# Order of the last sums and layout of the stores in a one-token decode block

## The chip, the cores and the metric

The kernel runs on one core of a Trainium2 chip. The core has a matrix engine (PE; its weight loads, PEld, are listed apart from its matmuls), VectorE (DVE), ScalarE (ACT), GpSimd (POOL) and SyncE (SP), which here issues all transfers between HBM and the on-chip memory SBUF. Matmuls write to PSUM, from which DVE or ACT copy. The metric is the device time of one execution in microseconds.

## The reference

A decode step for 8 sequences of one token each, model width 1024, all in float32. Two residual blocks follow each other:

```python
h  = x + A(layernorm(x), k_cache, v_cache, wq, wo)
h2 = h + B(layernorm(h), w_gate, w_up, w_down)

# A: 32 query heads of 128, 4 key/value heads, the last W = 1024 positions of a cache of 4096
q = (x @ wq) in heads;  p = softmax(q k^T * 128 ** -0.5);  A = (p v) @ wo
# B: width 3584
B = (gelu_tanh(x @ w_gate) * (x @ w_up)) @ w_down
```

The 8 tokens are few against the weights and the cache, some 111 MB that are read once.

## The kernel before, in words

**Tiling.** The 8 tokens are the stationary side of nearly every matmul, the weights the moving side. A matmul takes 32 stationary columns, and four of them, in the four groups of 32 columns of the PE array, run beside each other and write rows 0-31, 32-63, 64-95 and 96-127 of a PSUM bank. As there are 8 tokens, each stands four times in the 32 columns (`CP = 4` copies). The order of these columns is (copy, token): column 8 r + b is copy r of token b, so each group's rows in PSUM hold the 8 tokens four times over, copy after copy.

**Loads.** Two buffers of 64 KB in each partition take the weights in turn (`load`, line 119): two halves of wq, of K, of V and of wo, four blocks of w_gate and w_up, then w_down. A load is issued by SyncE when the matmuls that read the buffer before are done (`free`).

**The attention half** (lines 202-330): layernorm, query projection, scores, softmax, values, output projection. The output projection works in pairs: groups 0 and 1 take an even row chunk of 128 rows (left and right 512 output columns), groups 2 and 3 the odd one, so that the bank holds two partial sums. `add2`, a stationary matrix of zeros and ones, adds the two halves in a matmul (line 326). The residual sum goes to `h_sb` (line 329), whose rows 0-7 are the tokens and whose other rows are zero.

**The feed-forward half.** `layernorm_t` (line 173) normalizes `h_sb`, transposes it, and copies it out four times over (line 198), which gives the stationary tiles `ht`. Lines 335-362 make gate and up products, GELU and the transposed product `at`: 28 chunks of 128 rows, each with its 32 columns. w_down has 28 row chunks as well. They arrive in pieces of 8, 8, 4, 4, 2 and 1 chunks (`PARTS`), and the last chunk in three blocks, 128, 64 and 64 columns of each quarter of the output (`ENDS`). All are issued by line 391.

**The last sums** (lines 394-435), which the change touches. With `TAIL = 4`, `first` is 24 and `last` 27:

1. Chunks 0 to 23 go in pairs into bank `ya` (line 397), 512 columns at a time.
2. DVE copies `ya` to `d1` in SBUF (line 404).
3. `add` (line 410) sends one operand to the final sums: eight matmuls of 128 columns, four into `acc` and four into `tb`. Group j has the output quarter j (256 columns), of which `acc` holds the first 128 and `tb` the others. In this order `add` is called for the residual (`spread` selects row b of `h_sb` for each column of token b; this call opens the sums), for chunks 24 and 25, for `d1` with `add2`, and for chunk 26.
4. Chunk 27 follows in its three end blocks (line 429). ACT copies `acc` to `o_fin` when the first block is in, DVE copies `tb` when the third is in (line 433), and SyncE stores each half (lines 436-437): 128 rows of 128 numbers, contiguous in the output.

The order on each engine is the order of the source. An engine runs its instructions in that order, and `Flow` (line 31) puts a semaphore wait ahead of one only if what it needs isn't known to be done. Each `matmul` call of the source is two matmul instructions and two weight loads in the trace.

Of the kernel before, what the change touches and what calls it, by code (L numbers as in the profile page):

```python
# [2 lines left out]
F32 = mybir.dt.float32  # L3
# [4 lines left out]
P = 128  # L8
B = 8
# [5 lines left out]
NC = D // P  # L15
NQ = 4
CP = 32 // B
QW = D // NQ
N = 512
SET = NQ * N  # L20
HB = B // 2
SETS = (NQ, DF // N - NQ)
# [2 lines left out]
PARTS = (8, 8, 4, 4, 2, 1)  # L25
HEAD = 16
ENDS = (128, 64, 64)
TAIL = 4


class Flow:
# [42 lines left out]
    def run(self, engine, make, *waits, mark=True):  # L74
        ins = self.start(engine, make, waits)
        if not mark:
            return None
        self.done[engine] += 1
        ins.then_inc(self.own[engine], 1)
        return self.own[engine], self.done[engine]  # L80

    def move(self, name, out, src, *waits, engine="sync"):
        s = self.sem(name)
        self.start(engine, lambda e: e.dma_start(out, src), waits).then_inc(s, 16)  # L84
        return s, 16


def decode_block(nc, x, wq, kt, v, wo, gu, dn, ends, outs):
# [9 lines left out]
    run, move = fl.run, fl.move  # L98
# [4 lines left out]
    def sb(name, *shape):  # L103
        return nc.alloc_sbuf_tensor(name, list(shape), F32).ap()
# [14 lines left out]
    def load(src, name, letters, **sizes):  # L119
# [9 lines left out]
    ta, tb, ya = bank("ta", N), bank("tb", N), bank("ya", N)  # L129
    acc = bank("acc", N)  # L130

    x_sb = sb("x_sb", B, D)
    wq_t = [load(wq[0], "wq0", "c n", c=NC)]
    x_in = move("x", x_sb, x)
# [3 lines left out]
    ident = sb("ident", P, P)  # L138
    z = run("gpsimd", lambda e: e.memset(ident, 0.0))
    id_ok = run("gpsimd", lambda e: e.affine_select(  # L140
        out=ident, in_=ident, compare_op=ALU.not_equal, fill=1.0, base=0,
        pattern=[[-1, P]], channel_multiplier=1), z)
# [4 lines left out]
    h_sb = sb("h_sb", P, D)  # L147
    zero = [run("gpsimd", lambda e, t=t: e.memset(t, 0.0)) for t in (*qz, h_sb)]

    spread = sb("spread", P, CP, B)  # L150
    run("gpsimd", lambda e: e.tensor_copy(
        spread, ident[:, 0:B].unsqueeze(1).to_broadcast([P, CP, B])), id_ok)

    add2 = sb("add2", P, 2, 32)
    consts = run("gpsimd", lambda e: e.tensor_add(
        add2.rearrange("p c m -> p (c m)"), ident[:, 0:2 * 32], ident[:, 2 * 32:4 * 32]))
# [3 lines left out]
        out=own, in_=ident.rearrange("p (a b h) -> p b a h", b=HB, h=REP), axis=AX.XY,  # L160
# [9 lines left out]
                id_ok, ready, clear, mark=(i == n - 1))  # L170
        return t, tok

    def layernorm_t(src, ready, name, clear):

        bn = sb(name + "_bn", B, D // N, 6)
        tok = None
        for i in range(D // N):
            tok = run("vector", lambda e, i=i: e.bn_stats(bn[:, i], src[:, i * N:(i + 1) * N]), ready)
        mv, ve, sd, r0, r1, r2, rs = (
            sb(f"{name}_{n}", B, k) for n, k in  # L180
            (("mv", 2), ("ve", 1), ("sd", 1), ("r0", 1), ("r1", 1), ("r2", 1), ("rs", 1))
        )
        tok = run("vector", lambda e: e.bn_aggr(mv, bn), tok)
        tok = run("vector", lambda e: e.tensor_scalar(ve, mv[:, 1:2], EPS, None, op0=ALU.add), tok)  # L184
        tok = run("scalar", lambda e: e.activation(sd, ve, AF.Sqrt), tok)  # L185
        tok = run("vector", lambda e: e.reciprocal(r0, sd), tok)

        tok = run("vector", lambda e: e.scalar_tensor_tensor(
            r1, r0, r0, ve, op0=ALU.mult, op1=ALU.mult), tok)
        tok = run("vector", lambda e: e.tensor_scalar(  # L190
            r2, r1, -0.5, 1.5, op0=ALU.mult, op1=ALU.add), tok)
        tok = run("vector", lambda e: e.tensor_mul(rs, r0, r2), tok)
        xn = sb(name + "_xn", B, D)
        tok = run("vector", lambda e: e.tensor_scalar(  # L194
            xn, src, mv[:, 0:1], rs, op0=ALU.subtract, op1=ALU.mult), tok)
        pt, tok = transposes(ta, xn, NC, tok, clear, B)
        xt = sb(name + "_t", P, NC, CP, B)
        tok = run("vector", lambda e: e.tensor_copy(  # L198
            xt, pt.unsqueeze(2).to_broadcast([P, NC, CP, B])), tok)
        return [xt[:, c].rearrange("p r b -> p (r b)") for c in range(NC)], tok  # L200

    xt, x_ok = layernorm_t(x_sb, x_in, "ln1", None)
    ta_free = x_ok


    q_ok = []
    for hf in range(2):
        w, w_in, wb = wq_t[hf]
        q_ps = (acc, tb)[hf]
        for c in range(NC):  # L210
            for j in range(NQ):
                tok = run("tensor", lambda e, c=c, j=j: e.matmul(  # L212
                    q_ps[32 * j:32 * j + 32, :], xt[c], w[:, c, j * N:(j + 1) * N],
                    start=(c == 0), stop=(c == NC - 1)),
                    w_in, x_ok, mark=(c == NC - 1 and j == NQ - 1))
        free[wb] = tok
        q_sb = sb(f"q{hf}", P, N)
        tok = run("vector", lambda e: e.tensor_scalar(q_sb, q_ps, scale, None, op0=ALU.mult), tok)
        acc_free = tok
        qt, tok = transposes(ta, q_sb, N // P, tok, ta_free)  # L220

        for s in range(2):
            ta_free = run("vector", lambda e, s=s: e.tensor_copy(
                qz[hf][:, s].rearrange("p (b m) -> p b m", b=B)[:, :, 0:REP].rearrange(
                    "p b (k i) -> p b k i", k=2),
                qt.rearrange("p i (s k m) -> p s m k i", s=2, k=2)[:, s, 0:B]), tok, zero[hf])
# [4 lines left out]
    for hf in range(2):  # L231
        s_ps = big[hf]
        k_t, k_in, wb = load(kt[hf], f"kt{hf}", "s b k", s=2, b=B)
        for b in range(HB):
            for k0 in range(0, W, N):
                for r in range(NQ):
# [3 lines left out]
                    tok = run("tensor", lambda e: e.matmul(  # L240
                        s_ps[32 * r:32 * r + 32, k0:k0 + N], qz[hf][:, s, c0:c0 + 32],
                        k_t[:, s, half * HB + b, k0:k0 + N],
                        start=(b == 0), stop=(b == HB - 1)), k_in, q_ok[hf], mark=end)
# [29 lines left out]
    ya_free = None  # L273
    o_ps = (acc, tb)
    for hf in range(2):
        p_sb, p_ok, share, sh_ok = ps[hf]
        pt = sb(f"pt{hf}", P, KC, P)
        p0, tok0 = transposes(ta, p_sb[:, 0:W // 2], KC // 2, p_ok, ta_free)
        ta_free = run("vector", lambda e: e.tensor_copy(pt[:, 0:KC // 2, :], p0), tok0)
        p1, tok1 = transposes(ya, p_sb[:, W // 2:W], KC // 2, p_ok, ya_free)  # L280
        ya_free = run("scalar", lambda e: e.copy(pt[:, KC // 2:KC, :], p1), tok1)
        v_t, v_in, wb = load(v[hf], f"v{hf}", "s c b d", s=2, c=KC, b=B)
        o3 = o_ps[hf].rearrange("p (b d) -> p b d", b=HB)
        for c in range(KC):
            for r in range(NQ):
                s, half = divmod(r, 2)
                tok = run("tensor", lambda e: e.matmul(  # L287
                    o3[32 * r:32 * r + 32], pt[:, c, 32 * r:32 * r + 32],
                    v_t[:, s, c, half * HB:(half + 1) * HB, :],
                    start=(c == 0), stop=(c == KC - 1)),  # L290
                    v_in, ta_free, ya_free, mark=(c == KC - 1 and r == NQ - 1))
        free[wb] = tok
        o_sb = sb(f"o{hf}", P, DH)
        tok = run("vector", lambda e: e.tensor_scalar(
            o_sb, o3[:, 0], share[:, 0:1], None, op0=ALU.mult), tok, sh_ok)
        for b in range(1, HB):
            tok = run("vector", lambda e: e.scalar_tensor_tensor(
                o_sb, o3[:, b], share[:, b:b + 1], o_sb, op0=ALU.mult, op1=ALU.add), tok)
        if hf == 0:
            o_first = (o_sb, tok)  # L300
        else:
            ta_free = heads_out(0, *o_first, ta_free)
# [22 lines left out]
    for ch in range(2):  # L325
# [2 lines left out]
            ya_free, consts, ps[0][1], mark=(ch == 1))  # L328
    h_ok = run("vector", lambda e: e.tensor_add(
        h_sb[0:B], x_sb, big[0][0:B]), tok, zero[2])  # L330
    ht, ht_ok = layernorm_t(h_sb[0:B], h_ok, "ln2", ta_free)
    ta_free = ht_ok


# [42 lines left out]
    def rows_of(q):  # L377
        return chunks(q)[1][:, 0]
# [10 lines left out]
    for i, (n, src) in enumerate(zip(ENDS, ends)):  # L389
        t = rows_of(last)[:, NQ * c0:NQ * (c0 + n)]  # L390
        blocks.append((c0, n, t, move(f"we{i}", t, src)))
        c0 += n

    for q in range(0, first, 2):
        for r in range(NQ):
            e2, ch = divmod(r, 2)
            tok = run("tensor", lambda e: e.matmul(  # L397
                ya[32 * r:32 * r + 32, :], at[:, q + e2, :],
                rows_of(q + e2)[:, ch * N:(ch + 1) * N],
                start=(q == 0), stop=(q == first - 2)),  # L400
                arrived[q + e2], at_ok[(q + e2) * P >= SETS[0] * N], ya_free,
                mark=(q == first - 2 and r == NQ - 1))
    d1 = sb("d1", P, N)
    d1_ok = run("vector", lambda e: e.tensor_copy(d1, ya), tok)


    cut = ENDS[0]
    halves = [(acc[:, 0:cut], 0, cut), (tb[:, 0:QW - cut], cut, QW)]
# [1 line left out]
    def add(lhs, rhs, *waits, start=False):  # L410

        for d_ps, a, b in halves:
            for j in range(NQ):
                run("tensor", lambda e: e.matmul(  # L414
                    d_ps[32 * j:32 * j + 32, :], lhs(j), rhs(j)[:, a:b], start=start, stop=False),
                    *waits, mark=False)

    add(lambda j: spread.rearrange("p r b -> p (r b)"), lambda j: h_sb[:, j * QW:(j + 1) * QW],
        h_ok, consts, start=True)
    for q in range(first, last):  # L420
        add(lambda j: at[:, q, :], lambda j: rows_of(q)[:, j * QW:(j + 1) * QW], arrived[q], at_ok[1])
        if q == first + 1:
            add(lambda j: add2[:, j // 2, :], lambda j: d1[:, (j % 2) * QW:(j % 2) * QW + QW], d1_ok)
    o_fin = sb("o_fin", P, QW)
    done = []
    for i, (c0, n, t, here) in enumerate(blocks):
# [5 lines left out]
        if c0 + n == b:  # L432
            make = (lambda e: e.copy(o_fin[:, a:b], d_ps)) if i == 0 else (
                lambda e: e.tensor_copy(o_fin[:, a:b], d_ps))
            done.append(run(("scalar", "vector")[i > 0], make, tok))
    sent = [move("out0", outs[0], o_fin[:, 0:cut], done[0]),
            move("out1", outs[1], o_fin[:, cut:QW], done[1])]
    for s, val in sent:
        nc.sync.wait_ge(s, val)

# [76 lines left out]
```

## Time and profile before

| | |
|---|---|
| time, median of three runs | 267.58 us (265.7, 267.58, 268.12) |
| profiled execution: time | 267.58 us |
| profiled execution: span, first to last instruction | 266.3 us |
| PE matmuls, weight loads | 990 and 990, busy 51% and 15% of the span |
| mean granted TensorE clock | 0.788 |
| bytes moved | 111.45 MB, mean 419 GB/s |
| instruction queue q8 | 8 packets, 0.13 MB |
| each of the two stores | 64 KB |

In the fences below, a row of the chain has its start, its length and what it was (a DMA tile, or an engine with tile and line). A row of the timeline has start, length, engine, line, operation, tiles, shapes and the number of instructions, and in brackets the engine's idle time before it and what ended it. A row of the windows has start:end, length, then for PE, PEld, DVE, ACT and POOL the busy time with instructions in brackets, the granted clock, the DMA share of 16 engines and GB/s. A row of the issues ends in KB and in the time from issue to landing. A row of a DMA queue has packets, MB, and the share of 16 engines' time in the stretch asked for.

### The profile page before, as it was taken

How to read it: one execution, taken by the hardware profiler on the slowest of the kernel's cores; microseconds unless marked ns; L12 is line 12 of the kernel's file. 1: busy time of each engine (PE TensorE's matmuls, PEld its weight loads, DVE VectorE, ACT ScalarE, POOL GpSimd, SP SyncE). 2: the span in 40 equal slices, each digit the busy share in tenths (PEclk: the TensorE clock that was granted, in tenths of full speed). 3: DMA queues.
4: the chain of work that ended last, by engine and by line, in shares of the span. 5: the costliest groups of instructions: out<-in, count | busy, mean ns of one | idle time of the engine just before them, and what ended most of it. 6: DMA issues, size and time to landing. Idle time of an engine off the chain costs nothing.

```text
span 266.3 us, 2117 instructions
## 1 busy us (share of the span) xinstructions
PE 136.2 (51%) x990; PEld 40.1 (15%) x990; DVE 23.5 (9%) x55; ACT 10.5 (4%) x15; POOL 3.2 (1%) x11
## 2 busy tenths in 40 slices
PE   0000986805905806807708409619319294783874
PEld 0000321201201302202102102112002021120223
DVE  0004010100010110300300100250000200010000
ACT  1002000000010110110000000020000000000000
POOL 4000000000000000000000000000000000000000
PEclk9999995965865965975957956956858859599599
DMA  8997999799979997999799989998999989999992
GB/s 315 473 473 320 473 473 455 335 463 473 463 335 463 465 463 345 465 453 473 345 453 463 465 354 443 463 473 354 436 404 465 473 362 436 448 418 421 433 391 70
DMA packets 3338, 111.45 MB, mean 419 GB/s; under 512 B 377, under 2 KB 889, under 8 KB 1153
## 3 DMA queue, kind: packets, MB, share of 16 engines
q1 hardware_dynamic: 3328, 111.31, 97.4%
q8 instruction: 8, 0.13, 0.2%
q14 instruction: 2, 0.01, 0.0%
HBM read 111.18 MB, written 0.13 MB: 418 GB/s over the span
## 4 chain that ended last, share of the span: by engine, by line
DMA 76%; PE 22%; SPq 1%; issue 0%; DVE 0%
DMA w<-gu 19%; DMA w<-wq 15%; DMA w<-kt 11%; DMA w<-v 11%; DMA w<-wo 11%; DMA w<-dn 8%; PE big L345 7%; PE tb L212 4%; PE tb L287 4%; PE ya L315 3%; PE big L240 3%; SPq L84 1%; PE acc L414 0%; PE tb L414 0%; PE tb L429 0%
## 5 line engine op out<-in xcount | busy, mean ns | idle before, releaser
L345 PE MATMUL big<-w,ln_t 128*32 128x512 f32 x224 | 36.7, 737 | 20.9 <-DMA w<-gu 20.9
L240 PE MATMUL big<-w,qz 128*32 128x512 f32 x128 | 18.1, 728 | 19.3 <-DMA w<-kt 19.3
L315 PE MATMUL ya<-w,ot 128*32 128x512 f32 x128 | 17.3, 701 | 20.3 <-DMA w<-wo 20.3
L168 PE MATMUL ta<-ident,ln_xn 8*128 8x8 f32 x16 | 2.0, 251 | 31.6 <-DVE ln_xn L194 31.6
L397 PE MATMUL ya<-w,at 128*32 128x512 f32 x96 | 13.6, 717 | 7.0 <-DMA w<-dn 7.0
L345 PEld LDWEIGHTS big<-w,ln_t 128*32 128x32 f32 x224 | 9.1, 133 | 47.1 <-issue 25.8
L287 PE MATMUL tb<-w,pt 128*32 128x512 f32 x64 | 9.5, 761 | 9.4 <-DMA w<-v 9.4
L287 PE MATMUL acc<-w,pt 128*32 128x512 f32 x64 | 9.0, 727 | 9.8 <-DMA w<-v 9.8
L212 PE MATMUL tb<-w,ln_t 128*32 128x512 f32 x64 | 9.8, 779 | 2.7 <-DMA w<-wq 2.7
L212 PE MATMUL acc<-w,ln_t 128*32 128x512 f32 x64 | 10.0, 797 | 0.5 <-DVE ln_t L198 0.5
L315 PEld LDWEIGHTS ya<-w,ot 128*32 128x32 f32 x128 | 4.9, 127 | 31.3 <-issue 31.3
L240 PEld LDWEIGHTS big<-w,qz 128*32 128x32 f32 x128 | 4.7, 131 | 32.1 <-issue 22.3
L168 PEld LDWEIGHTS ta<-ident,ln_xn 8*128 8x128 f32 x16 | 1.8, 213 | 32.5 <-DVE ln_xn L194 32.5
L356 DVE TENSOR_TENSOR hm<-ge,big 128x512 f32<-128x512 f32 (+1 forms) x2 | 1.4, 686 | 56.8 <-PE big L345 56.8
L397 PEld LDWEIGHTS ya<-w,at 128*32 128x32 f32 x96 | 3.2, 129 | 16.6 <-DMA w<-dn 8.8
L249 DVE TENSOR_REDUCE nmax<-big 128x1 f32<-128x1024 f32 x2 | 2.4, 1224 | 34.1 <-PE big L240 34.1
L287 PEld LDWEIGHTS tb<-w,pt 128*32 128x32 f32 x64 | 2.6, 135 | 15.7 <-issue 15.7
L287 PEld LDWEIGHTS acc<-w,pt 128*32 128x32 f32 x64 | 2.5, 131 | 15.7 <-issue 15.7
L251 ACT ACTIVATE p<-big,nmax 128x1024 f32<-128x1024 f32 x2 | 2.2, 1114 | 64.9 <-DVE nmax L249 64.9
L212 PEld LDWEIGHTS tb<-w,ln_t 128*32 128x32 f32 x64 | 2.4, 139 | 9.4 <-issue 6.5
L185 ACT ACTIVATE ln_sd<-ln_ve 8x1 f32<-8x1 f32 x2 | 0.4, 202 | 83.8 <-DVE ln_ve L184 83.8
L212 PEld LDWEIGHTS acc<-w,ln_t 128*32 128x32 f32 x64 | 2.4, 140 | 7.4 <-issue 6.8
(73 smaller groups left out, 51.1 us busy)
## 6 DMA issues: line engine op xcount, KB each, us to landing
w<-gu SPq DMA_DIRECT2D x2, 6144.0 KB, 22.4
w<-dn SPq DMA_DIRECT2D x2, 4096.0 KB, 19.2
w<-dn SPq DMA_DIRECT2D x2, 2048.0 KB, 17.3
w<-dn SPq DMA_DIRECT2D x1, 1024.0 KB, 21.6
w<-dn SPq DMA_DIRECT2D x1, 512.0 KB, 22.4
w<-ends SPq DMA_DIRECT2D x1, 256.0 KB, 22.5
w<-ends SPq DMA_DIRECT2D x2, 128.0 KB, 22.3
out<-o_fin SPq DMA_DIRECT2D x2, 64.0 KB, 2.4
```

Of the source, the lines that this page charges most:

```text
L84: self.start(engine, lambda e: e.dma_start(out, src), waits).then_inc(s, 16)
L168: tok = run("tensor", lambda e, i=i: e.transpose(t[:, i, :], src[:, i * P:(i + 1) * P], ident[:rows, :rows]), id_ok, ready, clear, mark=(i ...
L185: tok = run("scalar", lambda e: e.activation(sd, ve, AF.Sqrt), tok)
L212: tok = run("tensor", lambda e, c=c, j=j: e.matmul(q_ps[32 * j:32 * j + 32, :], xt[c], w[:, c, j * N:(j + 1) * N], start=(c == 0), stop=(c ...
L240: tok = run("tensor", lambda e: e.matmul(s_ps[32 * r:32 * r + 32, k0:k0 + N], qz[hf][:, s, c0:c0 + 32], k_t[:, s, half * HB + b, k0:k0 + N ...
L249: tok = run("vector", lambda e: e.tensor_reduce(out=nmax, in_=s_ps, axis=AX.X, op=ALU.max, negate=True), tok)
L251: p_ok = run("scalar", lambda e: e.activation(p_sb, s_ps, AF.Exp, bias=nmax, accum_out=tot), tok)
L287: tok = run("tensor", lambda e: e.matmul(o3[32 * r:32 * r + 32], pt[:, c, 32 * r:32 * r + 32], v_t[:, s, c, half * HB:(half + 1) * HB, :], ...
L315: tok = run("tensor", lambda e: e.matmul(ya[32 * r:32 * r + 32, :], ot[:, 2 * hf * REP + h + e2].rearrange("p r b -> p (r b)"), w[:, h + e ...
L345: tok = run("tensor", lambda e: e.matmul(pair[32 * j:32 * j + 32, s, :], ht[c], w[:, c, j * N:(j + 1) * N], start=(c == 0), stop=(c == NC ...
L356: tok = run("vector", lambda e: e.tensor_mul(hm[:rows], ge[:rows], pair[:rows, 1, :]), tok, g_ok)
L397: tok = run("tensor", lambda e: e.matmul(ya[32 * r:32 * r + 32, :], at[:, q + e2, :], rows_of(q + e2)[:, ch * N:(ch + 1) * N], start=(q == ...
```

## The change

`TAIL` becomes 2, so `first` is 26: chunks 24 and 25 join the pairs, and only chunks 26 and 27 go one by one. The residual is no longer the first of the final sums. It opens the pairs' sum instead, with two matmuls of 512 columns in groups 0 and 1 of `ya`, ahead of the first pair; groups 2 and 3 are opened by the first odd chunk. So `d1` now holds the residual and chunks 0 to 25. The final sums are opened by chunk 26, then take `d1` by `add2`, then the three end blocks.

The 32 columns of the second layernorm's output are in the order (token, copy), column 4 b + r, by an argument of `layernorm_t`; `spread` likewise. The first layernorm keeps (copy, token). In the final sums, rows 4 b of each group of 32 are then copy 0 of token b, and each store takes every fourth of the 128 rows: 32 rows of 128 numbers, 16 KB, into an output of 32 rows of 256.

```diff
-TAIL = 4
+TAIL = 2
...
-    spread = sb("spread", P, CP, B)
+    spread = sb("spread", P, B, CP)
     run("gpsimd", lambda e: e.tensor_copy(
-        spread, ident[:, 0:B].unsqueeze(1).to_broadcast([P, CP, B])), id_ok)
+        spread, ident[:, 0:B].unsqueeze(2).to_broadcast([P, B, CP])), id_ok)
...
-    def layernorm_t(src, ready, name, clear):
+    def layernorm_t(src, ready, name, clear, order):
...
-        xt = sb(name + "_t", P, NC, CP, B)
+        xt = sb(name + "_t", P, NC, CP * B)
         tok = run("vector", lambda e: e.tensor_copy(
-            xt, pt.unsqueeze(2).to_broadcast([P, NC, CP, B])), tok)
-        return [xt[:, c].rearrange("p r b -> p (r b)") for c in range(NC)], tok
+            xt.rearrange(f"p c ({order}) -> p c r b", b=B),
+            pt.unsqueeze(2).to_broadcast([P, NC, CP, B])), tok)
+        return [xt[:, c] for c in range(NC)], tok
-    xt, x_ok = layernorm_t(x_sb, x_in, "ln1", None)
+    xt, x_ok = layernorm_t(x_sb, x_in, "ln1", None, "r b")
...
-    ht, ht_ok = layernorm_t(h_sb[0:B], h_ok, "ln2", ta_free)
+    ht, ht_ok = layernorm_t(h_sb[0:B], h_ok, "ln2", ta_free, "b r")
...
+    for ch in range(2):
+        run("tensor", lambda e: e.matmul(
+            ya[32 * ch:32 * ch + 32, :], spread.rearrange("p b r -> p (b r)"),
+            h_sb[:, ch * N:(ch + 1) * N], start=True, stop=False), h_ok, consts, ya_free, mark=False)
     for q in range(0, first, 2):
         for r in range(NQ):
             e2, ch = divmod(r, 2)
             tok = run("tensor", lambda e: e.matmul(
                 ya[32 * r:32 * r + 32, :], at[:, q + e2, :],
                 rows_of(q + e2)[:, ch * N:(ch + 1) * N],
-                start=(q == 0), stop=(q == first - 2)),
-                arrived[q + e2], at_ok[(q + e2) * P >= SETS[0] * N], ya_free,
+                start=(q == 0 and e2 == 1), stop=(q == first - 2)),
+                arrived[q + e2], at_ok[(q + e2) * P >= SETS[0] * N],
                 mark=(q == first - 2 and r == NQ - 1))
...
-    add(lambda j: spread.rearrange("p r b -> p (r b)"), lambda j: h_sb[:, j * QW:(j + 1) * QW],
-        h_ok, consts, start=True)
     for q in range(first, last):
-        add(lambda j: at[:, q, :], lambda j: rows_of(q)[:, j * QW:(j + 1) * QW], arrived[q], at_ok[1])
-        if q == first + 1:
-            add(lambda j: add2[:, j // 2, :], lambda j: d1[:, (j % 2) * QW:(j % 2) * QW + QW], d1_ok)
+        add(lambda j: at[:, q, :], lambda j: rows_of(q)[:, j * QW:(j + 1) * QW],
+            arrived[q], at_ok[1], h_ok, start=(q == first))
+    add(lambda j: add2[:, j // 2, :], lambda j: d1[:, (j % 2) * QW:(j % 2) * QW + QW], d1_ok)
...
-    sent = [move("out0", outs[0], o_fin[:, 0:cut], done[0]),
-            move("out1", outs[1], o_fin[:, cut:QW], done[1])]
+    sent = [move("out0", outs[0], o_fin[0:P:CP, 0:cut], done[0]),
+            move("out1", outs[1], o_fin[0:P:CP, cut:QW], done[1])]
...
-    out = nc.dram_tensor("out", (P * QW,), F32, kind="ExternalOutput").ap()
-    cut = P * ENDS[0]
-    outs = [o.rearrange("(p n) -> p n", p=P) for o in (out[0:cut], out[cut:P * QW])]
+    out = nc.dram_tensor("out", (NQ * B, QW), F32, kind="ExternalOutput").ap()
+    outs = [out[:, 0:ENDS[0]], out[:, ENDS[0]:QW]]
```

More of the change, by code (lines that the diff above doesn't have):

```diff
@@ L511 @@
     r = run_bass_kernel_spmd(nc, [arrays], core_ids=[0])
-    flat = r.results[0]["out"].reshape(-1)
-    got = np.concatenate(
-        [flat[:cut].reshape(P, -1), flat[cut:].reshape(P, -1)], axis=1
-    ).reshape(NQ, CP, B, QW)[:, 0]
+    got = r.results[0]["out"].reshape(NQ, B, QW)
     return own(got.transpose(1, 0, 2)).reshape(B, 1, D)
```

## The prediction

> **What bounds the kernel now.** I read the page first: its totals, the chain that ended last, and the DMA queues.
>
> ```profile
> span 266.3 us, 2117 instructions
> PE 136.2 (51%) x990; PEld 40.1 (15%) x990; DVE 23.5 (9%) x55; ACT 10.5 (4%) x15; POOL 3.2 (1%) x11
> ...
> q8 instruction: 8, 0.13, 0.2%
> ...
> DMA 76%; PE 22%; SPq 1%; issue 0%; DVE 0%
> ```
>
> The weight stream ends last almost everywhere; PE is busy half the span. Every change lies in the last 30 us, so next comes the chain cut to its end.
>
> ```profile
> 237.91 21.58 DMA w<-dn
> ...
> 259.54 0.42 PE acc L414 x8
> ...
> 261.50 0.34 PE acc L429 x8
> 261.84 0.60 PE tb L429 x16
> 262.46 0.29 DVE o_fin L434
> ```
>
> The chain waits for rows 24 and 25 of w_down until 259.50, then is PE work until 261.84 + 0.60 = 262.44, one copy, and the store (which this view leaves out). The instructions of that stretch, in order of time:
>
> ```profile
> 257.02 1.92 PE L397 MATMUL ya<-w,at 128*32 128x512 f32 x16 [1.77 <-DMA w<-dn]
> 257.48 0.13 PEld L397 LDWEIGHTS ya<-w,at 128*32 128x32 f32 x4 [0.30 <-issue]
> 257.91 0.13 PEld L397 LDWEIGHTS ya<-w,at 128*32 128x32 f32 x4 [0.30 <-issue]
> ...
> 258.76 0.40 PE L414 MATMUL acc<-h_sb,spread 128*32 128x128 f32 x8
> ...
> 259.02 0.69 DVE L404 COPY d<-ya 128x512 f32<-128x512 f32 x1 [19.99 <-PE ya L397]
> 259.54 0.16 PEld L414 LDWEIGHTS acc<-w,at 128*32 128x32 f32 x8 [0.43 <-DMA w<-dn]
> ...
> 260.00 0.40 PE L414 MATMUL acc<-w,at 128*32 128x128 f32 x8
> ...
> 260.44 0.40 PE L414 MATMUL acc<-d,add 128*32 128x128 f32 x8
> ...
> 260.80 0.21 PEld L414 LDWEIGHTS acc<-w,at 128*32 128x32 f32 x8
> 260.88 0.40 PE L414 MATMUL acc<-w,at 128*32 128x128 f32 x8
> ...
> 261.41 0.16 PEld L429 LDWEIGHTS acc<-w,at 128*32 128x32 f32 x8 [0.19 <-DMA w<-ends]
> ...
> 261.80 0.44 PEld L429 LDWEIGHTS tb<-w,at 128*32 128x32 f32 x16 [0.23 <-DMA w<-ends]
> 261.91 0.27 ACT L433 COPY o_fin<-acc 128x128 f32<-128x128 f32 x1 [38.34 <-PE acc L429]
> 262.08 0.16 PEld L429 LDWEIGHTS tb<-w,at 128*32 128x32 f32 x8
> ```
>
> What to see: PE isn't late here. It waits for the first end block until 261.41 and for the second until 261.80; the first eight loads of the pair end at about 261.96, so the third block's eight, at 262.08, waited about 0.1 us for it. Loads and PE finish within a few tenths of each other. The copy of the pairs' sum (259.02 to 259.71) is done long before its use at 260.44. Last, the two stores: their issues, a view of each issue with its time to landing, the traffic from 262.7 to 266.3 in 40 slices of 0.09 us, and the instruction queue from 263.5 to 266.3.
>
> ```profile
> 262.20 0.35 SPq L84 DMA_DIRECT2D out<-o_fin  x1
> ...
> 262.78 0.34 SPq L84 DMA_DIRECT2D out<-o_fin  x1
> ...
> out<-o_fin SPq DMA_DIRECT2D x1, 64.0 KB, 1.5
> ...
> out<-o_fin SPq DMA_DIRECT2D x1, 64.0 KB, 3.3
> ...
> GB/s 0 0 0 23 210 302 171 23 0 0 302 279 216 160 0 0 0 0 0 0 0 0 0 0 0 6 6 11 6 11 6 0 0 0 0 0 0 0 0 0
> ...
> q8 instruction: 1, 0.02, 3.2%
> ```
>
> This is the largest thing in the tail. The first store lands after 1.5 us, the second, equal in size, after 3.3: at 262.78 + 3.3 = 266.1, the end of the span. Its bytes move in slices 10 to 13 (263.6 to 264.0), except some at 6 to 11 GB/s in slices 25 to 30 (265.0 to 265.4): 46 GB/s x 0.09 us = 4 KB, a sixteenth of its 64 KB, one engine's share. In the same stretch one packet of the instruction queue takes 3.2% of 16 engines x 2.8 us = 1.43 us. I read it as an instruction fetch that got onto one engine just ahead of its share, from 263.6 to 265.0. Without it the second store, like the first, would land after about 1.5 us, at 264.3: the fetch costs **1.8 us**.
>
> **The change part by part.** Per matmul of the source the trace has two instructions.
>
> *Instructions.* Four adds of 16 become none, the residual becomes 4 wide instructions, and one pair of rows adds 8: removed are residual, row 24 and row 25 (48), added 12. That is 36 matmuls and 36 weight loads fewer, **72** on PE. When are instructions fetched? The first row below is the queue from 46.4 to 46.8 (the first fetch; there is none before), the second the queue over 0 to 255, the third PE's counts from there to PE's end.
>
> ```profile
> q8 instruction: 1, 0.02, 16.7%
> ...
> q8 instruction: 6, 0.10, 0.2%
> ...
> 46.50:262.40 215.90, 120.42 (x898) 35.40 (x890) 18.38 (x40) 7.70 (x12) 0.00 (x0) 0.75 0.99 425
> ```
>
> From the first fetch to the eighth PE starts 1,788 instructions, 1,788 / 7 = 255 for each fetch; the fetches keep step with PE. The eighth comes 1.4 us after PE's last weights. If it is due on PE's count, it falls just past the end of PE's work now, and with 72 fewer it is due 72 instructions later than PE has any: it disappears from the span, at a gain between 0 and 1.8 us. If instead it belongs to PE reaching its end, it stays: gain 0. I take the count, because seven intervals average to a constant, and 1.8 us. [...]
>
> *Residual ahead of the pairs.* Its 4 instructions of 512 columns cost between 0.43 us (four weight loads are 0.43 apart at L397: 257.48 to 257.91) and 1.88 (four serial ones, below); they fill two column groups, so I take 1.0. They start at about 238.4 and delay the first eight chunks, behind which stands idle time:
>
> ```profile
> 169.11 0.69 DVE L323 COPY y_sb<-ya 128x512 f32<-128x512 f32 x1 [18.92 <-PE ya L315]
> 169.95 1.88 PE L326 MATMUL big<-y_sb,add 128*32 128x512 f32 x4 [0.90 <-DVE y_sb L323]
> 241.60:247.20 5.60, 0.41 (x4) 0.00 (x0) 0.00 (x0) 0.00 (x0) 0.00 (x0) 0.88 0.94 404
> 247.20:252.60 5.40, 5.37 (x28) 1.39 (x32) 0.00 (x0) 0.00 (x0) 0.00 (x0) 0.50 0.98 419
> 254.90:257.00 2.10, 0.35 (x4) 0.00 (x0) 0.00 (x0) 0.00 (x0) 0.00 (x0) 1.00 1.03 419
> ```
>
> PE has 0.41 us left of the first eight chunks after 241.6 and is then idle for 5.2 us until 247.2, so the cost is 0. At its old place it also ran during a wait (idle 0.43 before 259.54), so its removal gains 0.
>
> *Rows 24 and 25 as a pair.* Two adds take 0.88 (259.54 to 260.44, less the first start's 0.02); as a pair two groups of eight at 0.43 per four, 0.86. The work is equal: 259.54 + 0.86 = 260.40. But the copy of the sum now waits for it. Now it starts 0.26 after the next work's start (258.76 to 259.02): 260.66 to 261.35. Row 26, here by 260.80, takes 0.44 meanwhile, to 261.24. Behind the copy PE holds the two-part sum and, in order, all end blocks. From the copy's end to the matmul is 0.15 (169.80 to 169.95): 261.50, and 0.44 for its 16 (260.44 to 260.88): the first end block starts at **261.94 instead of 261.41, +0.53**. Half an add later, 262.16, comes the second block; its eight instructions of 64 columns take some 0.11, the third block starts at 262.27 instead of about 262.10: **+0.17**, since the loads took part of the delay anyway. ScalarE's copy ends at 262.71, DVE's at 262.92.
>
> *Stores.* The first is issued at 262.73. SyncE is then busy for 0.35 + 0.04, so the second goes at 263.12 instead of 262.78: **+0.34** (0.17 if the first were not in the way). Each has 16 KB in 32 rows instead of 64 KB in 128. The four slices of the second's bytes, 0.36 us, shrink to one at best: between 0 and 0.27, I take **-0.15**; a spread over fewer engines or the step of four rows could eat that, and is in the zero.
>
> *Columns as (token, copy).* GpSimd's small copy near the start has 230 us before use. The transposed ln2 copy writes at a step of four:
>
> ```profile
> 177.82 0.42 DVE L198 COPY ln_t<-ta 128x256 f32<-128x256 f32 x1 [1.11 <-PE ta L168]
> ...
> 179.47 1.08 PE L345 MATMUL big<-w,ln_t 128*32 128x512 f32 x4 [1.69 <-DMA w<-gu]
> ```
>
> It ends at 178.24 and PE waits for weights until 179.47. Between equal and four times as long (1.7 us), I take equal, nearest to the row; at four times 0.05 us would show, and the next load would have to wait for it.
>
> *Sum.* +0.34 - 0.15 - 1.8 = -1.6. The span goes from 266.3 to 264.7; the profiled execution's time, 267.58, is 1.28 above its span, and is also the median of the three. 264.7 + 1.3 = **266.0**. (The lowest of the three, 265.7, may be one that the fetch missed; no trace of it is shown.)
>
> **The rivals.** *The fetch stays*, because PE's end, not the count, calls it. It comes after PE's last work, 0.17 later, and holds its engine to about 265.15; two packets instead of eight (0.45 us in slices 25 to 30) end 0.11 later, 265.26 against 265.43. So -0.15: **267.4**. For it: the fetch follows PE's end by 1.4 us, and all the kernel's PE instructions have been started by then, so the count must go on in something that the profile doesn't list. Against: the even 255.
>
> *The clock is lost in the tail*, which makes it slower. The rows above show full clock kept over 2.1 us of idle (1.00) and lost in the 5.2 us before 247.2 (0.88 of 5.6: the last 1.3 us at half, from 245.9), then half clock until 252.6. The residual shortens that idle by a microsecond. If the clock then holds, rows 8 to 19 take 12 x 0.43 = 5.2 us and are done at 252.5, and PE idles 4.5 us until 257.0. If the gate closes there, the tail runs at half speed for the 5.3 us seen at 247.2: rows 20 to 25 take 6 x 0.85 from 257.02, to 262.14; copy from 262.40 to 263.09, sum at 263.24, end block at 263.68, 1.74 after my 261.94. That is **267.7** with the fetch gone, and **269.1**, slower than before, with it still there. It decides at an idle time of some 3.9 us (242.0 to where the clock fell, 245.9). For it: 4.5 lies above that. Against: the clock must first hold through the shortened gap of 4.2 us, which lies above it too. [...]
>
> *The change buys nothing that ends last*: the fetch arrives a little later than the packets by itself and the stores' size doesn't matter: 265.7 to 266.2, inside the forecast.
>
> **How the numbers follow.** The forecast, 266.0, has 0.58; the fetch that stays 0.20; the lost clock 0.14 (0.09 without, 0.05 with the fetch); 0.08 is for what no row shows. The forecast's own bounds: store and SyncE terms from -0.27 + 0.17 to 0 + 0.39 put it between 265.7 and 266.2, and runs of one kernel differ by 2.4 us (265.7 to 268.12), about one either way. The range, 265.0 to 268.0, takes in the forecast, the fetch that stays and the milder clock case. Over 1% (what measuring this kernel can tell from no change) is 2.7 us: under 264.9 takes the forecast and a lucky spread, 0.10; over 270.3 takes the worst clock case and more, 0.06; within, 0.84.
>
> **What would show it.** Right: seven packets on the instruction queue up to the end of the stores, the second store landing in about 1.4 us, the copy of the sum at about 260.7, the end block's weights without a wait for their load, 72 fewer PE instructions. Wrong: an eighth packet with one engine's bytes late; half clock after 257; a store in which few engines work.

## The result and the profile after

The change makes no difference. Over 20 executions each, the changed kernel has a median of 267.69 us (266.91 to 268.67) and the kernel before 267.65 (265.7 to 269.58); the ratio is 1.0008, 95% interval 0.9989 to 1.0028. The forecast was 266.0, with a range from 265.0 to 268.0; the measured time lies inside the range, but the gain that was forecast isn't there.

The two sets of values look different, though. Before: five of 20 at 265.7 to 266.0, the others scattered up to 269.6. After: nine at 266.9 to 267.2, ten at 267.7 to 268.0, one at 268.67, and none below. Neither the best nor the worst executions of the kernel before are among those of the changed one. The profiled execution of the changed kernel took 266.96 us. Its page:

```profile
span 265.6 us, 2045 instructions
...
PE 136.5 (51%) x954; PEld 39.2 (15%) x954; DVE 23.7 (9%) x55; ACT 10.5 (4%) x15; POOL 3.2 (1%) x11
...
q8 instruction: 7, 0.11, 0.2%
...
DMA 76%; PE 22%; SPq 1%; issue 0%; DVE 0%
```

PE has 72 instructions fewer, and the instruction queue q8 has seven packets instead of eight, as forecast. The end in order of time:

```profile
259.46 1.06 PE L406 MATMUL ya<-w,at 128*32 128x512 f32 x8 [0.71 <-DMA w<-dn]
260.60 0.69 DVE L413 COPY d<-ya 128x512 f32<-128x512 f32 x1 [22.08 <-PE ya L406]
...
260.72 0.43 PE L422 MATMUL acc<-w,at 128*32 128x128 f32 x8 [0.19 <-DMA w<-dn]
...
261.34 0.16 PEld L422 LDWEIGHTS acc<-d,add 128*32 128x32 f32 x8 [0.25 <-DVE d L413]
261.35 0.43 PE L422 MATMUL acc<-d,add 128*32 128x128 f32 x8
...
261.81 0.40 PE L435 MATMUL acc<-w,at 128*32 128x128 f32 x8
...
262.02 0.41 PE L435 MATMUL tb<-w,at 128*32 128x64 f32 x16
262.27 0.27 ACT L439 COPY o_fin<-acc 128x128 f32<-128x128 f32 x1 [39.22 <-PE acc L435]
262.50 0.29 DVE L440 COPY o_fin<-tb 128x128 f32<-128x128 f32 x1 [1.21 <-PE tb L435]
262.56 1.17 SPq L84 DMA_DIRECT2D out<-o_fin  x2
```

The weight loads of the two-part sum now wait for the copy of the pairs' sum (260.60 to 261.29), and no end block is waited for. Row 26, which PE could start only at 260.72, when its load had landed, keeps PE busy until 261.36, so the copy and row 26 end together. The two halves of the output become ready 0.25 us apart (262.54 and 262.79), where before they were 0.57 apart (262.18 and 262.75). The stores, in the views used for before: the first issue, the landing of the first and the median of both, SyncE's wait for them, the traffic from 263.1 to 265.6 in slices of 0.0625 us, and the other instruction queue, q14, from 264.0 to 264.2:

```profile
262.56 0.54 SPq L84 DMA_DIRECT2D out<-o_fin  x1
...
out<-o_fin SPq DMA_DIRECT2D x1, 16.0 KB, 1.7
...
out<-o_fin SPq DMA_DIRECT2D x2, 16.0 KB, 2.0
...
SPq L446 <- DMA out<-o_fin: 1.8, 1, 1.8
...
GB/s 0 0 0 0 0 0 0 0 0 0 98 91 66 8 0 0 131 0 0 0 57 107 74 17 8 0 0 0 0 0 0 0 0 0 0 0 0 0 0 0
...
q14 instruction: 1, 0.01, 15.5%
```

An issue keeps SyncE 0.54 us instead of 0.35, so the second starts at 262.56 + 1.17 - 0.58 = 263.15. Its bytes start at slice 20, 264.35, 1.2 us after the issue (0.85 before). With a median of 2.0 and 1.7 for the first, the second takes 2.3 us to land, not the 1.35 of the forecast. Each store has 16 landings in the records, one of each part, and they show where the time goes: 15 of 16 have landed by 264.95, the last at 265.49. Between the two stores stands a packet of 131 GB/s x 0.0625 us = 8 KB (slice 16), a fetch on q14, 15.5% of 16 engines x 0.2 us = 0.5 us long. The kernel before has a packet of this kind too, from 263.93 to 264.60. Here is its queue from 263.5 to 266.3:

```profile
q14 instruction: 1, 0.01, 1.5%
```

There the bytes of the second store, except those behind the 16 KB fetch, were out by 263.97, and 15 of its parts landed by 264.32. **So one fetch at the end is gone, and the later store now meets another that was there already.**

### The profile page after: what moved, and what is told of

Same layout as the page of the kernel before. It is cut to its first block, busy times and chain, and to the rows that moved or that the text cites. A ratio compares the mean times of both kernels' runs of the same rounds, so it can differ in the third digit from the quotient of the medians.

```text
span 265.6 us, 2045 instructions
## 1 busy us (share of the span) xinstructions
PE 136.5 (51%) x954; PEld 39.2 (15%) x954; DVE 23.7 (9%) x55; ACT 10.5 (4%) x15; POOL 3.2 (1%) x11
## 4 chain that ended last, share of the span: by engine, by line
DMA 76%; PE 22%; SPq 1%; issue 0%; DVE 0%
DMA w<-gu 19%; DMA w<-wq 15%; DMA w<-kt 12%; DMA w<-wo 11%; DMA w<-v 11%; DMA w<-dn 9%; PE big L349 7%; PE big L244 4%; PE tb L291 3%; PE tb L216 3%; PE ya L319 3%; SPq L84 1%; PE acc L422 0%; PE tb L422 0%; DVE o_fin L440 0%
## 5 line engine op out<-in xcount | busy, mean ns | idle before, releaser
L244 PE MATMUL big<-w,qz 128*32 128x512 f32 x128 | 19.4, 775 | 19.9 <-DMA w<-kt 19.9
L319 PE MATMUL ya<-w,ot 128*32 128x512 f32 x128 | 18.3, 737 | 19.3 <-DMA w<-wo 19.3
L406 PE MATMUL ya<-w,at 128*32 128x512 f32 x104 | 15.1, 694 | 7.5 <-DMA w<-dn 7.5
L216 PE MATMUL tb<-w,ln_t 128*32 128x512 f32 x64 | 8.8, 711 | 3.1 <-DMA w<-wq 3.1
```

Source lines behind the costliest of these rows:

```text
L216: tok = run("tensor", lambda e, c=c, j=j: e.matmul(q_ps[32 * j:32 * j + 32, :], xt[c], w[:, c, j * N:(j + 1) * N], start=(c == 0), stop=(c ...
L244: tok = run("tensor", lambda e: e.matmul(s_ps[32 * r:32 * r + 32, k0:k0 + N], qz[hf][:, s, c0:c0 + 32], k_t[:, s, half * HB + b, k0:k0 + N ...
L319: tok = run("tensor", lambda e: e.matmul(ya[32 * r:32 * r + 32, :], ot[:, 2 * hf * REP + h + e2].rearrange("p r b -> p (r b)"), w[:, h + e ...
L406: tok = run("tensor", lambda e: e.matmul(ya[32 * r:32 * r + 32, :], at[:, q + e2, :], rows_of(q + e2)[:, ch * N:(ch + 1) * N], start=(q == ...
```

## The experiments

The first theory, A: the fetch is gone and the new stores give the gain back. Its rival, B: the longer chain or the clock gives it back.

**The changed kernel with full stores.**

```diff
-    sent = [move("out0", outs[0], o_fin[0:P:CP, 0:cut], done[0]),
-            move("out1", outs[1], o_fin[0:P:CP, cut:QW], done[1])]
+    sent = [move("out0", outs[0], o_fin[:, 0:cut], done[0]),
+            move("out1", outs[1], o_fin[:, cut:QW], done[1])]
```

> The changed kernel, but it stores all 128 rows of each half in one contiguous piece, as the kernel before does. Theory A (the fetch is gone, and the stores of every fourth row give the gain back: their issue takes SyncE 0.54 to 0.58 us instead of 0.35 and their bytes start 1.2 us after the issue instead of 0.83): issue 0.35 again, the second store lands 1.5 us after it, span 264.9 in the profile, median 266.4, ratio to before 0.995. Theory B (the longer tail on PE, with the copy of the sum on the chain, or the clock in it gives the gain back): the same as the changed kernel, 267.6, ratio 1.000.

Measured: median 267.96, ratio 1.0027 (0.9994 to 1.0059). Theory A falls: the stores' form alone isn't it. The profile, an execution of 268.03, showed instead what the upper group is. Its windows, and the copy of the sum:

```profile
247.00:250.20 3.20, 3.20 (x16) 0.76 (x20) 0.00 (x0) 0.00 (x0) 0.00 (x0) 0.50 0.99 420
250.20:253.40 3.20, 3.20 (x36) 0.81 (x28) 0.00 (x0) 0.00 (x0) 0.00 (x0) 1.00 1.01 430
253.40:256.80 3.40, 0.54 (x12) 0.04 (x7) 0.00 (x0) 0.00 (x0) 0.00 (x0) 1.00 0.98 410
256.80:260.40 3.60, 3.60 (x20) 0.90 (x24) 0.00 (x0) 0.00 (x0) 0.00 (x0) 0.53 0.89 343
...
261.31 0.69 DVE L413 COPY d<-ya 128x512 f32<-128x512 f32 x1 [21.93 <-PE ya L406]
```

The clock came back at 250.2, PE had rows 8 to 19 done by 253.9, waited, and got half clock in the tail, from about 257.0 to 260.4 (0.53 over 3.6 us, which is some 3.4 us at half). The copy starts at 261.31 instead of 260.60. The prediction's rival of the lost clock exists. That the half clock isn't owed to the change is shown further down.

**The stores of every fourth row alone, on the kernel before** (with the (token, copy) columns; the residual and rows 24 and 25 as before).

> The kernel before with the (token, copy) columns and the stores of every fourth row alone; residual and rows 24 and 25 stay in the one-by-one adds. Theory A: eight instruction fetches as before, the issue of a store 0.54 us instead of 0.35, median 0.4 to 0.6 above before (ratio 1.002). Theory B (the stores' form is free or saves 0.15): ratio 0.999 to 1.000.

Measured: 267.27, ratio 0.9994 (0.9962 to 1.0026). Its page differs from before in one number that neither theory had, and a second profile of the kernel before shows the eighth packet again; both kernels have 2117 instructions and PE's 1980.

```profile
span 265.4 us, 2117 instructions
...
q8 instruction: 7, 0.11, 0.2%
```

> The kernel before once more, for a second profile. If PE's count calls the eighth 16 KB fetch, it stands again 1.4 us after PE's last weights; whether it meets the second store may differ. If not, it is absent, with a time near 265.7 when the clock was full in the tail.

Measured: one execution, 268.0 us. The eighth 16 KB fetch stands 1.4 us after PE's last matmul again, and the clock was at half from 258 to 261.2 here too (0.50). So the kernel before has both troubles, the fetch and the half clock, in some of its executions. Of the six at the granted clock 0.821, that of full_store's profile and of this one, among the 35 of the kernel before beside the first experiments, none took under 267.76.

**PE's count raised by 160 on the kernel before, by 72 on the changed one.** In both, small matmuls at the start, 40 here and 18 on the changed kernel:

```diff
+    for i in range(40):
+        run("tensor", lambda e: e.matmul(
+            ya[0:32, 0:8], ident[:, 0:32], ident[:, 0:8], start=True, stop=True), id_ok, mark=False)
     xt, x_ok = layernorm_t(x_sb, x_in, "ln1", None)
```

> The kernel before with 40 matmuls of 8 columns (160 PE instructions) added at its start, where PE waits 26 us for the first load; their result is used nowhere. If fetches go by PE's count, the eighth comes 160 instructions earlier, during the loads, and meets no store: the second store lands 1.5 us after its issue, median 265.9, the lowest values of the kernel before, ratio 0.994. If the last fetch belongs to PE's end, or if it costs the usual execution nothing: ratio 1.000.

> The changed kernel with 18 matmuls of 8 columns (72 PE instructions) added at its start, where PE waits for the first load, so that PE has as many instructions as before. By the count the eighth fetch is back at PE's end (8 packets on the instruction queue) and some executions are longer by up to 1.4 us: median 268.2, ratio 1.002. If PE's end alone decides: 7 packets and 267.7.

Measured: 266.76 for the first, six of 12 at 265.5 to 265.8 and six at 267.7 to 268.5, ratio 0.9981 (0.994 to 1.0021); the eighth fetch is at 260.9, in the loads. In the second, 267.69 and seven packets, though PE's count is that of before. So the fetch at PE's end can be moved by padding, but count alone doesn't foretell it: with 1980 PE instructions it is there in the kernel before, twice, and absent in two others. In the kernel before and in the one with the strided stores the seventh fetch even comes after the same 1740 PE instructions, and only the first has an eighth, behind the other 240.

**Who calls the q14 fetch: both last copies on ScalarE.**

```diff
-            make = (lambda e: e.copy(o_fin[:, a:b], d_ps)) if i == 0 else (
-                lambda e: e.tensor_copy(o_fin[:, a:b], d_ps))
-            done.append(run(("scalar", "vector")[i > 0], make, tok))
+            done.append(run("scalar", lambda e: e.copy(o_fin[:, a:b], d_ps), tok))
```

> The changed kernel with both last copies on ScalarE; VectorE's last instruction is the copy of the pairs' sum, 1.2 us earlier. Theory D (the 8 KB instruction fetch that delays one engine's share of the second store by 0.5 to 1.4 us in every profile of the short tail is called by VectorE's end, which it follows by 1.2 to 1.3 us): it comes at 262.5, before the stores' bytes, and all 16 parts of the second store land together; 0.5 less, median 267.1. If it is called by PE's end (1.75 to 1.9 us before it): unchanged, 267.7. If by ScalarE's end: later, past the stores' bytes, 0.5 less as well, and it stands 1.5 to 1.75 us after ScalarE's last copy.

Measured: 267.39, ratio 1.0006 (0.9982 to 1.0031). VectorE's last instruction ended at 261.24, and the fetch came at 264.08, 1.92 after PE's last matmul started. Theory D, that VectorE's end calls it, falls. If ScalarE's end called it, it should have come 1.5 to 1.75 after ScalarE's last copy and past the store's bytes; it came 1.37 after it and ahead of them.

**Work in PE's waits**, five matmuls whose result is used nowhere, on the changed kernel; and the same with 60 small ones at the start on the kernel before:

```diff
+    def fill(n):
+        for i in range(n):
+            run("tensor", lambda e: e.matmul(
+                big[1][0:32, 0:N], ident[:, 0:32], rows_of(0)[:, 0:N], start=True, stop=True),
+                at_ok[0], arrived[0], mark=False)
     for q in range(0, first, 2):
+        if q in (8, 20):
+            fill(3 if q == 8 else 2)
```

> The changed kernel with five matmuls of 512 columns, whose result is used nowhere, in the two waits of PE for rows 8 and 20 of w_down (2.6 and 1.7 us of PE work), so that no wait is long enough to lose the clock. If the values of 267.7 to 268.0 of the changed kernel, most of which have the granted clock 0.821, are executions whose tail runs at half clock, they go: median 267.0, no value above 267.4, no half clock between 247 and the end in the profile. If they come from the stores or the fetches, the median stays at 267.7.

> The kernel before with the same five matmuls in PE's waits, and 60 matmuls of 8 columns at its start, so that the eighth 16 KB fetch comes during the loads. If the spread of the kernel before (265.5 to 270.2) is made of a half clock in the tail and of fetches that meet the second store, both are gone: nearly all values 265.5 to 265.9, ratio 0.992. If one of them isn't the cause, values of 267.6 and above stay.

Measured on the changed kernel: ten of 12 at 266.85 to 267.16 and two above (267.89 and 270.28), median 267.05, and full clock (1.00) from 242 to the end in the profile. So the upper group, 0.8 above the lower, is the half clock in the tail. On the kernel before: 266.11, ratio 0.9961 (0.9935 to 0.9987); six of 12 at 265.6 to 265.94, five from 266.28 to 267.32 and one at 270.35, so not nearly all at 265.5 to 265.9, as expected. The padding of 60 had put a ninth fetch at PE's end, 1.4 us after its last matmul; in the profile it meets the second store. With padding of 40 instead both should go, and on that quiet base each part of the change could be tried by itself.

**The parts of the change on a quiet base.** `base40` is the kernel before with `fill` and 40 small matmuls. `resid46`, `pair52` and `strided40` each add one part of the change; padding of 46 and 52 keeps PE's count the same. The core of the second and third:

```diff
 resid46
+    for ch in range(2):
+        run("tensor", lambda e: e.matmul(ya[32 * ch:32 * ch + 32, :], ..., start=True, stop=False), ...)
-    add(lambda j: spread..., lambda j: h_sb[:, j * QW:(j + 1) * QW], h_ok, consts, start=True)
 pair52
-TAIL = 4
+TAIL = 2
-        if q == first + 1:
-            add(lambda j: add2[:, j // 2, :], ..., d1_ok)
+    add(lambda j: add2[:, j // 2, :], ..., d1_ok)
```

> The kernel before with the five matmuls in PE's waits and 40 small ones at its start: clock kept, and no 16 KB fetch at PE's end (as with 40 alone). If half clock and fetches make the spread of the kernel before: nearly all values 265.5 to 265.9, the second store's 16 parts land together, 1.5 us after its issue, span 264.3, ratio to before 0.992.

> base40 with the residual opening the pairs' sum and nothing else of the change (46 small matmuls keep PE's count). The residual ran in a wait at either place: as base40, 265.6. If its move costs, the values lie above that.

> base40 with rows 24 and 25 as a pair and nothing else of the change (52 small matmuls keep PE's count). By the sum of the prediction the copy of the sum delays the first end block by 0.53 and the second store by 0.2 to 0.35: 266.0. Theory E: both halves are then ready at nearly the same time, the second store waits behind the first one's issue, its bytes start later after PE's end and meet the 8 KB fetch that follows PE's end by 1.75 to 1.9 us, so that one engine's part lands another 1.2 later: 266.9 to 267.2.

> base40 with the (token, copy) columns and the stores of every fourth row and nothing else of the change. If the small stores save time: 265.4. Theory E: their issue takes SyncE 0.54 to 0.58 instead of 0.35 and their bytes start 1.2 us after it instead of 0.83, so they meet the same fetch: 266.6 to 267.0, as the lower values of the run with these stores alone.

Measured, 12 executions each, beside 267.70 for the kernel before:

| | median | lowest to highest | ratio to before |
|---|---|---|---|
| base40 | 265.71 | 265.44 to 266.24 | 0.9952 (0.9925 to 0.9979) |
| resid46 | 265.72 | 265.61 to 266.71 | 0.9952 (0.9925 to 0.9978) |
| pair52 | 267.22 | 266.8 to 267.44 | 0.9998 (0.997 to 1.0026) |
| strided40 | 266.70 | 266.44 to 267.6 | 0.9979 (0.9955 to 1.0003) |

The residual's move is free. The pair costs 1.5 us and the stores 1.0, where the prediction had +0.17 to +0.34 and -0.15. They don't add up: the changed kernel with filled waits, 267.05, lies 1.3 above base40, not 2.5. The last copy, an issue, its landing and the traffic from 262.6 to 266.0 in slices of 0.085 us, then the q14 fetch where it falls, for base40 (the issue is the second one, the last row from 263.75 to 263.9):

```profile
262.35 0.29 DVE L445 COPY o_fin<-tb 128x128 f32<-128x128 f32 x1 [2.77 <-PE tb L440]
...
262.67 0.34 SPq L84 DMA_DIRECT2D out<-o_fin  x1
...
out<-o_fin SPq DMA_DIRECT2D x1, 64.0 KB, 1.5
...
GB/s 0 0 0 0 151 313 235 73 0 0 36 241 295 175 121 0 0 0 0 0 0 0 0 0 0 0 0 0 0 0 0 0 0 0 0 0 0 0 0 0
...
q14 instruction: 1, 0.01, 28.2%
```

and for pair52 (both issues; the last row from 263.8 to 263.95):

```profile
262.39 0.29 DVE L444 COPY o_fin<-tb 128x128 f32<-128x128 f32 x1 [1.21 <-PE tb L439]
262.45 0.83 SPq L84 DMA_DIRECT2D out<-o_fin  x2
...
out<-o_fin SPq DMA_DIRECT2D x2, 64.0 KB, 2.2
...
GB/s 0 0 0 0 0 0 0 0 120 289 265 91 6 24 283 307 163 42 0 0 0 0 0 0 0 12 24 6 6 0 0 0 0 0 0 0 0 0 0 0
...
q14 instruction: 1, 0.01, 38.2%
```

PE and DVE end within 0.04 us of each other in the two. In base40 the second store's bytes end at slice 14 (263.8), when the 8 KB fetch begins. In pair52 SyncE is still issuing the first store when the second half is ready; the second starts at 262.85 instead of 262.67, its bytes 0.2 later, and a sixteenth of them (48 GB/s x 0.085 us = 4 KB) comes only behind the fetch (38.2% of 16 x 0.15 = 0.92 us), in slices 25 to 28 (264.7 to 265.1). Across profiles, from the records, in us after the start of PE's last matmul:

| | second store issued | its bytes start | 8 KB fetch starts | 15 parts landed | last part |
|---|---|---|---|---|---|
| base40 | 0.61 | 1.45 | 1.76 | 2.11 | 2.14 |
| pair52 | 0.75 | 1.68 | 1.76 | 2.37 | 3.65 |
| strided40 | 0.61 | 1.85 | 1.78 | 2.38 | 3.12 |
| changed kernel | 0.94 | 2.18 | 1.89 | 2.74 | 3.28 |

Most of the lost time is the last part, 0.5 to 1.3 us behind the others. This is theory E: a second store that has more than its last packets still to send when the 8 KB fetch starts has a part that lands late. The profile of the kernel before with padding of 40 (268.52) fits it as well: half clock from 258.7 to 262.1, stores issued 0.35 and 0.74 after PE's last matmul, the fetch at 1.84, and a last part 1.27 behind the others. So the kernel before meets the 8 KB fetch too, in an execution whose tail ran at half clock.

What the fetch does to the part isn't the same in all. In pair52 its bytes wait: the last eight packets of 512 bytes follow at 2.68, where the fetch ends. On the changed kernel the last bytes go out only 0.06 after the others and land 0.54 after them, and with its padding of 18 they aren't late at all, yet one part lands 0.5 behind. What holds back such a landing isn't shown. Two more kernels tried theory E from both sides.

```diff
 base40_late
+            if i > 0:
+                run("vector", lambda e: e.tensor_copy(late, d1[:, 0:64]), tok)
 pair52_actq
-    sent = [move("out0", outs[0], o_fin[:, 0:cut], done[0]),
+    sent = [move("out0", outs[0], o_fin[:, 0:cut], done[0], engine="scalar"),
```

> base40 with one small copy (64 columns, some 0.15 us) on VectorE ahead of the copy of the second half; its result is used nowhere. If being late against the fetch is what counts, the second store's bytes start 0.15 later, the fetch that follows PE's last matmul by 1.75 us gets ahead of one engine's share, and the cost is 1.2 to 1.5 us: 266.9 to 267.2. If a delay costs only itself: 265.9.

> pair52 with the first store issued by ScalarE, which makes that half; SyncE issues only the second. The second store is then issued as soon as its half is copied, 0.6 us after PE's last matmul as in base40, ahead of the fetch: 265.8 to 266.0. If the pair's order itself costs the time, 267.2 stays.

Measured, six executions each beside 268.05 for the kernel before. **pair52_actq: 265.78** (265.6 to 266.78), ratio 0.9923 (0.9896 to 0.9949). Its two issues and the second's landing:

```profile
262.36 0.37 ACTq L84 DMA_DIRECT2D out<-o_fin  x1
262.61 0.35 SPq L84 DMA_DIRECT2D out<-o_fin  x1
...
out<-o_fin SPq DMA_DIRECT2D x1, 64.0 KB, 1.6
```

The order of PE's work is pair52's and the 1.5 us are gone, so that order by itself isn't the cost. The second store is issued at 0.61 again, and all its words are out by 1.83 after PE's last matmul. But the fetch moved as well, to 2.08, 0.3 later than in pair52; the run doesn't tell the earlier store from the later fetch. base40_late came out at 265.95 (265.8 to 266.28), ratio 0.9926 (0.9899 to 0.9953), only 0.24 above base40, against the 266.9 to 267.2 of theory E. Its profile says that the trial missed its aim: the 8 KB fetch wasn't at the end any more but in the loads, from 242.3 to 242.6:

```profile
q14 instruction: 1, 0.01, 6.9%
...
262.51 0.20 DVE L448 COPY late<-d 128x64 f32<-128x64 f32 x1 [2.78 <-PE tb L441]
```

With one more VectorE instruction it had moved. So the trial doesn't show the jump, but it shows the other half. Its second store is issued at 0.71, its last words go out at 1.89, past the 1.76 at which base40's fetch starts, and all 16 parts land together, by 2.25 (2.14 in base40). With no fetch about, the store issued 0.10 later lands 0.11 later and no more. An early store with the fetch (base40), a late one without it (base40_late) and both together (pair52, strided40): among these the late part comes only with both. No single kernel was run with and without the fetch alone.

## Why the prediction was wrong

- **The work on PE and its chain: right.** Copy of the sum forecast at 260.66, measured 260.60; first end block 261.94, 261.81; DVE's last copy done at 262.92, 262.79. The residual ahead of the pairs cost nothing. One step is off: row 26 was to be done by 261.24 and leave the copy alone on the chain, but it waited for its load and ran to 261.36. ("Four adds of 16 become none" is a slip; the sum rightly takes three, 48.)
- **SyncE between the stores: right in size, partly by luck.** The second issue was forecast at 263.12 and came at 263.15; but the first was 0.17 earlier than forecast, and its issue 0.19 longer.
- **The fetch is gone: right for this kernel, its reason not.** Seven packets, as forecast. The count doesn't decide alone: two kernels with before's count have seven as well, and no row tells which kernel gets a fetch at the end. Nor is the 255 even, from which the count was my estimate: the seven intervals have 220 to 297 PE instructions.
- **The step that failed is the gain of 1.8 us,** "Without it the second store, like the first, would land after about 1.5 us", together with the stores' -0.15: the second store landed 2.3 us after its issue. The price of the 16 KB fetch was right where the second store stays early: base40, without that fetch, has a span of 264.4 against 266.3. But a landing of the second store after 1.5 us was seen only where its bytes are all but out when the 8 KB fetch starts, or where none comes. That fetch follows PE's last matmul by 1.75 to 1.92 in all profiles that have it at the end but one, pair52_actq's with 2.08. I added the +0.34 of delay as 0.34, as if nothing else were due behind it; in pair52 a delay of 0.14 (0.75 against 0.61) goes with that meeting and costs 1.5. The page listed that queue, q14, and I passed over it. Of the 0.9 us between the forecast span, 264.7, and the measured 265.6, 0.4 is the later start of the bytes (1.2 instead of 0.85 after the issue) and 0.5 the late part (265.49 against 264.95). The median lies another 0.7 above the profiled execution's 266.96, as about half of the executions have the half clock in the tail.
- **The rival of the lost clock was given 0.14 and priced at 1.74.** By the two groups of values it appears in about half of the changed kernel's executions, at 0.8; in the profile that shows it, full_store's, it lasted 3.4 us instead of the 5.3 taken. It isn't the change's: the kernel before has it too (0.50 from 258 to 261.2 in before_again's). The idle time of some 3.9 us at which it was to decide was my estimate from one profile, and no run shows it as a limit: PE had been idle for 2.86 us ahead of the half clock in full_store's profile and for 2.53 in before_again's. That the rival's 267.7 is the measured median is chance, as 0.9 of the miss is the second store and not the clock. So is the nearness of the 267.4 for the fetch that stays.
- **The base.** The 267.58 of the profile stood for a mixture. Without half clock and without a fetch that meets a store the kernel takes 265.7 (base40); the profiled executions that met the 16 KB fetch took 267.58 and, with half clock as well, 268.0. That the executions of the kernel before near 265.7 have neither wasn't seen in a trace. The changed kernel is rid of the 16 KB fetch and meets the 8 KB one instead, in each of its profiles, and none of its executions is near 265.7. That the two medians agree to 0.04 us is a balance of these, not a sign that nothing moved.

The four lowest medians of all are base40, 265.71, resid46, 265.72, pair52_actq, 265.78, and base40_late, 265.95, all with intervals below the kernel before. Their gain, 0.5% to 0.8% beside the executions of the kernel before that ran with each, comes with the filled waits and the padding that they share, and not from the change: base40 has no part of it.

What calls either fetch at the end stays open. Padding PE moves the 16 KB one; with one VectorE instruction more the 8 KB one was elsewhere, with one less it wasn't. The runs don't say more.

## What to carry to other kernels

Look at what lands last, part by part, and at the instruction queues beside it: the changed kernel's second store had 15 of its 16 parts landed by 264.95 and was done at 265.49. A delay of a tenth of a microsecond isn't priced at a tenth when something else is due in that gap (0.14 went with 1.5 in pair52); ask what the later transfer will meet. And when a kernel's executions lie 4 us apart, find out what the lowest ones lack before one profile is taken as the base.

## What the runs showed of the hardware that was not expected

- A store of every fourth row, 32 rows of 512 bytes into rows of 1024, kept SyncE 0.54 and 0.58 us in the changed kernel instead of 0.35 and 0.34 before, and its bytes started 1.2 us after the issue (changed kernel 1.20, strided40 1.24) instead of 0.84 to 0.93 (kernel before 0.85, base40 0.84, pair52 0.93), though it moves a quarter of the bytes.
- One 8 KB instruction packet took 0.33 us in the loads (base40_late) and 0.43 to 0.92 at the end (strided40 0.43, changed kernel 0.50, base40 0.68, pair52 0.92). One of 16 KB took 1.02 to 1.10 in the loads and 1.44 at the end of the kernel before. Where one started while a store had more than its last packets to send, one of the store's 16 parts landed 0.5 to 1.8 us after the others (changed kernel 0.54, strided40 0.74, pair52 1.28, kernel before 1.80). That part and packet share one DMA engine is an estimate from the 4 KB of 64 that are late in pair52 and in the kernel before; the records don't name the engine.
- Half clock in the last 10 us came and went between executions of one kernel: of the kernel before's two profiles, one has the 0.50 of 258 to 261.2 and the other has full clock there. With five matmuls in two waits of PE (2.7 and 1.9 us in the changed kernel's profile) no profile whose clock was read shows it up to PE's end (1.00 from 236 to 264 in after_warm and before_warm), and the changed kernel's median, 267.05, stayed within its lower group, 266.9 to 267.2.
